# Where attention's ten weight conversions stand, and how many products of zeros open the kernel

## The chip, the cores and the metric

One of the eight cores of a Trainium2 chip runs the whole program. The metric is the time of one execution on the device in microseconds (us). The engines are TensorE (PE in the profile; its weight loads are PEld), VectorE (DVE), ScalarE (ACT), GpSimd (POOL) and SyncE (SP). Each engine works through its own instructions in a fixed order; an instruction whose input isn't there holds up all that stand behind it.

## The reference

Three layers follow each other. Attention has 4 batches, 8 heads, 576 positions and head width 64: the scores are `q k^T / 8`, a bias from the cumulated sums of `max(s, 0)` is added and clipped, the causal mask and a softmax follow, and the result is multiplied by `v`. The output, as 2304 rows of 512, goes through a layer of width 2048:

```python
h = x @ w_in
g = h * (1.0 / (1.0 + np.exp(-1.702 * h)))
x = g @ w_out
```

and then through a second one of the same sizes, with a rational function `P(h) / (Q(h) + 1e-6)` in place of the gate. The weights arrive as 64-bit floats.

## The kernel before

**Attention.** It is cut into 80 units: four batches, in each four pairs of heads, in each pair five tiles of rows, in the order 0, 1, 4, 2, 3. The loop in `attention` makes one step `j` per unit: it issues the scores of unit `j` (L289 on PE, the masked minimum L319 on DVE, the exponential L326 on ACT, the scaling by the inverse sum L339 on POOL), the transposes of unit `j - 3` (L360, L364, L381, copied out of PSUM at L361, L365, L385, L388) and the products with `v` of finished units (L406). In each pair the next pair's `k` and `q` are turned (L225) and split into a high and a low part (L213 on ACT, L216 on DVE, for the first two pairs moved by POOL at L251).

**Filler.** From batch 1 on PE has more to do than attention: `fill` deals out the first layer's work for the batch before (`mlp1_first`) in portions, three times per step. It begins at `j = 24`, with the products of the first five slices `f` of `w_in` (L638, with the gate at L649, L650, L652 and L655) for two halves of the rows, and then the products with the same five slices of `w_out` (`out1`, L662), from step 32 on: in each accumulation slice 0 comes first and slice 4 last, the first time at the end of step 33. Before `j = 24` `fill` only issues products of zeros (`warm`, L82) in the first five steps.

**Conversions.** The five slices need ten conversions of 128 x 512 weights from 64-bit floats to a high and a low 32-bit part (`convert`): the five halves of `w_in` first, then the five of `w_out` (`CONV`). One conversion is three instructions on ACT (L558, L560, and L566 that writes the high part), three on DVE (L561, L562, L563) and two on POOL (L565, and L567 that writes the low part). `emit` issues one after each step named in `CONV_J`. The raw weights come by a DMA on SP's queue (L547, L549) into one of three slots.

**Order.** In attention PE's order is the order of the code. On the other engines a scheduler places the instructions when the program is built. The eight PSUM banks serve all of it in turn.

**After attention.** The rest of the first layer and the second layer follow, with PE at work nearly all the time.

Of the kernel before, what the change touches and what calls it, by code (L numbers as in the profile page):

```python
# [47 lines left out]
PT_W = (256, 512, 768, 1024)  # L48
PARTS = ((0, 256), (256, 576))
ZEROS = 5  # L50
WARM = 6
RUN_ENDS = ((0, 1, 4, 2, 3), (4, 3), (4, 3), (3,))
W2_SLOTS = 7
LEAD = 2
CONV_J = (4, 6, 9, 12, 15, 18, 21, 24, 27, 30)
CONV = [(f, 0) for f in range(F1)] + [(f, 1) for f in range(F1)]
STG = 1536
BT_BUFS, G_BUFS = 9, 9
# [3 lines left out]
class Fused:  # L62
# [136 lines left out]
    def prep(self, att, b, p, ld, first=False):  # L199
# [48 lines left out]
        def move(o, i, hs=(0, 1)):  # L248
            if g < 2:
                for h in hs:  # L250
                    self.copied = nc.gpsimd.tensor_copy(o[:, h], i[:, h].bitcast(F32))  # L251
            else:
                nc.sync.dma_start(o.bitcast(F32), i.bitcast(F32))

        if first:
            turned = [[turn(nm, h) for nm in "kq"] for h in range(2)]
            for h in range(2):
# [7 lines left out]
                move(k2[h0, 1], qs[h0], (h,))  # L265
            self.warm(WARM)
            return
# [165 lines left out]
    def attention(self, att, mlp):  # L433
# [30 lines left out]
        for j in range(n + AHEAD + 1):  # L464
            i, k = j - AHEAD, j - AHEAD - 1
            self.zeros = j < ZEROS
            tr = iter(())
            if j < n:
                b, p, t = units[j]
                idx = j % 5  # L470
                if idx == 0 and units[j][1:] != (NP - 1, 0) or (idx == 0 and b + 1 < NB):
                    nprep = self.prep(att, *divmod(b * NP + p + 1, NP), loads.pop(b * NP + p + 1))
            if i >= 0 and i < n and units[i][0] and i % 20 == 1:
                self.filler = chain(self.filler, self.mlp1_first(mlp, units[i][0] - 1))
                self.cold = False
            q = FILL / 20
            if j < n:
                self.unit_scores(att, units[j], 0)
                if j:
                    next(nprep, None)  # L480
                if j == 2:
                    with self.behind((opened,)):
                        later.pop(0)()
                    with self.behind((self.moved,)):
                        self.raw_ahead()
            self.fill(q / 3, 1 if j else 4)
            if 0 <= i < n:
                tr = self.unit_transpose(att, units[i])
                next(tr, None)
            if j < n:  # L490
                self.unit_scores(att, units[j], 1)
            self.fill(q / 3, j < 4)
            for _ in tr:
                pass
            if j < n and idx == 4:
                for _ in nprep:
                    pass
                g = b * NP + p
                g = {0: 3, 1: 4, 2: NB * NP}.get(g, g + 2)
                if g < NB * NP:  # L500
                    with self.behind((opened,)):
                        loads[g] = self.pair_load(att, *divmod(g, NP))
                    later.append(loads[g]["values"])
            if k >= 0:
                run.append(units[k])
                if units[k][2] in RUN_ENDS[units[k][0]]:
                    for u in run:
                        self.unit_values(att, u)
                    run.clear()
                if units[k][2] == 3 and later:  # L510
                    later.pop(0)()
            self.fill(q / 3, j < 4)
            if j == AHEAD_J[0]:
                self.stg_n, self.stg_k = 0, 2
                buf = self.stg_slot[:, 2 * STG : 2 * STG + 1024].bitcast(F32R)
                buf = buf.rearrange("p (i f) -> p i f", i=2)
                for f in AHEAD_F:
                    for half in range(2):
                        self.task(
                            lambda st, f=f, half=half: self.park(st, buf, 1, f, half), 1, f, half  # L520
                        )
            if j in COEF_J:
                with self.behind((*self.tail, self.moved)):
                    if j == COEF_J[0]:
                        self.coefficients()
                    else:
                        self.nc.scalar.activation(self.cf[:, 6:8], self.cf[:, 4:6], AF.Abs)
            if j in CONV_J or j in AHEAD_J:
                with self.behind((*self.tail, opened)):
                    self.emit(1)  # L530
# [479 lines left out]
```

## Time and profile before

| | |
|---|---|
| three runs | 1022.36, 1023.72, 1023.92 us; median 1023.72 us |
| profiled execution | 1023.65 us, of which its span is 1021.7 us |
| PE busy | 1002.8 us, 98% of the span |
| DVE, ACT, POOL busy | 796.5, 718.8, 337.0 us |
| chain that ended last | PE 91%, DVE 4%, ACT 2%, DMA 1%, issue 1% |

The span runs from the first to the last instruction; the execution's own time is 1.95 us longer. The chain is followed back from the last instruction to what released each, so its shares say which engine the end waited for. A mean over the whole span hides that the first 80 us are another stage than the rest, so most rows below are of single stretches.

### The profile page before, as it was taken

Reading aid. Unit: us, or ns where it says so; the run is one execution under the profiler, and the core shown is the slowest. Engines: PE = TensorE matmul, PEld = TensorE weight load, DVE = VectorE, ACT = ScalarE, POOL = GpSimd, SP = SyncE. Lnnn points to the kernel's source line nnn. Section 1 sums busy time; section 2 is a strip of 40 time slices with the busy share of each in tenths; the row PEclk is TensorE's granted clock in tenths of the full one; section 3 lists DMA queues with packets and bytes.
Section 4 is the critical chain, followed back from the end, with each engine's and each line's share of the span. In section 5 each row is a group of like instructions: output and inputs, shape, how many; then the busy total and the mean of one; then the engine's idle time right before and its main releaser. Section 6 shows DMA issues by size and latency. Waiting matters only on the chain.

```text
span 1021.7 us, 19825 instructions
## 1 busy us (share of the span) xinstructions
PE 1002.8 (98%) x7053; PEld 936.4 (92%) x7054; DVE 796.5 (78%) x1804; ACT 718.8 (70%) x1661; POOL 337.0 (33%) x503
## 2 busy tenths in 40 slices
PE   8899999999999999999999999999999999999997
PEld 5678999999999999999999999999999999989896
DVE  7897667665537977777778747999998989889886
ACT  5999889878756655555555436777887777777775
POOL 5778656545410012222111112223222222222222
PEclk8999999999999999999999999999999999999999
DMA  7664465552228646766657635010010100100000
GB/s 182 150 166 104 131 179 148 153 140 72 53 97 274 183 126 197 234 222 231 222 176 239 207 124 208 1 31 32 1 62 1 32 31 1 63 1 1 32 1 31
DMA packets 79074, 115.97 MB, mean 114 GB/s; under 512 B 25552, under 2 KB 63072, under 8 KB 77440
## 3 DMA queue, kind: packets, MB, share of 16 engines
q1 hardware_dynamic: 72640, 94.94, 31.4%
q0 software_dynamic: 6112, 19.47, 5.1%
q8 instruction: 56, 0.92, 0.4%
q14 instruction: 42, 0.34, 0.1%
q10 hardware_dynamic: 224, 0.30, 0.1%
HBM read 74.78 MB, written 31.60 MB: 104 GB/s over the span
## 4 chain that ended last, share of the span: by engine, by line
PE 91%; DVE 4%; ACT 2%; DMA 1%; issue 1%; POOL 0%; ACTq 0%; SPq 0%; DVEq 0%
PE h L638 39%; PE a L815 19%; PE a L662 19%; PE s L289 5%; PE O L406 4%; PE tp L381 3%; DVE bt L319 1%; PE tk L225 1%; DMA x2p<-st 1%; PE tq L225 1%; PE tp L360 1%; DVE k L216 1%; PE idle L82 0%; ACT bt L326 0%; DMA raw<-in_moe_w_out_dram 0%
## 5 line engine op out<-in xcount | busy, mean ns | idle before, releaser
L638 PE MATMUL h<-x,u 128*128 128x288 f32 x1536 | 231.5, 296 | 1.0 <-ACT st L677 1.0
L662 PE MATMUL a<-gh,u 128*128 128x288 f32 x1024 | 231.8, 297 | 0.0
L638 PEld LDWEIGHTS h<-x,u 128*128 128x128 f32 x1536 | 212.8, 188 | 3.0 <-ACT st L677 1.3
L798 POOL TENSOR_TENSOR gl<-u,gh 128x384 fp32r<-128x384 f32 x96 | 105.6, 1100 | 289.8 <-ACT gh L796 265.5
L662 PEld LDWEIGHTS a<-gh,u 128*128 128x128 f32 x1024 | 173.0, 188 | 1.4 <-issue 0.5
L638 PE MATMUL h<-y,u 128*128 128x384 f32 x864 | 165.7, 336 | 0.0
L638 PEld LDWEIGHTS h<-y,u 128*128 128x128 f32 x864 | 152.9, 188 | 6.2
L662 PE MATMUL a<-gl,u 128*128 128x288 f32 x512 | 150.0, 295 | 0.1
L815 PE MATMUL a<-u,gh 128*128 128x512 f32 x432 | 114.6, 394 | 0.9 <-ACT gh L796 0.9
L649 ACT ACTIVATE g<-h 128x288 f32<-128x288 f32 x128 | 52.1, 408 | 78.5 <-PE h L638 77.8
L724 POOL DMA_DIRECT2D x<-xp x64 | 35.2, 551 | 207.4 <-DVE g L650 107.1
L662 PEld LDWEIGHTS a<-gl,u 128*128 128x128 f32 x512 | 96.5, 188 | 0.9 <-DVE gl L655 0.4
L326 ACT ACTIVATE bt<-bt,mn 128x128 f32<-128x128 f32 (+2 forms) x144 | 84.0, 584 | 18.6 <-DVE mn L319 17.3
L815 PEld LDWEIGHTS a<-u,gh 128*128 128x128 f32 x432 | 80.0, 188 | 14.9 <-ACT gh L796 1.8
L339 POOL TENSOR_SCALAR bt<-bt,sm 128x128 f32<-128x128 f32 (+2 forms) x144 | 81.7, 579 | 29.4 <-DVE sm L336 21.4
L796 ACT ACTIVATE gh<-u 128x384 fp32r<-128x384 f32 x96 | 50.6, 527 | 57.9 <-DVE u L794 57.9
L319 DVE CUSTOM_DVE_ANT_0 bt<-s,mask 128x128 f32<-128x128 f32 (+2 forms) x144 | 68.9, 481 | 28.3 <-PE s L289 26.4
L652 ACT ACTIVATE gh<-g 128x288 fp32r<-128x288 f32 x128 | 56.5, 443 | 45.4 <-DVE g L650 43.8
L650 DVE SCALAR_TENSOR_TENSOR g<-g,h 128x288 f32<-128x288 f32 x128 | 57.5, 450 | 30.1 <-ACT g L649 29.5
L781 ACT ACTIVATE y<-h,cf 128x384 f32<-128x384 f32 x96 | 55.4, 577 | 33.3 <-PE h L638 33.3
L786 DVE SCALAR_TENSOR_TENSOR y<-s,cf,y 128x384 f32<-128x384 f32 x96 | 59.2, 617 | 20.2 <-ACT s L783 18.8
L794 DVE SCALAR_TENSOR_TENSOR u<-y,u 128x384 f32<-128x384 f32 x96 | 73.4, 765 | 1.1
(116 smaller groups left out, 2054.2 us busy)
## 6 DMA issues: line engine op xcount, KB each, us to landing
raw<-in_moe_w_in_dram SPq DMA_DIRECT2D x24, 512.0 KB
raw<-in_moe_w_out_dram SPq DMA_DIRECT2D x24, 512.0 KB
x<-xp POOLq DMA_DIRECT2D x64, 144.0 KB, 3.0
wd<-park POOLq DMA_DIRECT2D x36, 256.0 KB, 4.4
u<-wd SPq DMA_DIRECT2D x8, 1024.0 KB
x2p<-st SPq DMA_DIRECT2D x32, 144.0 KB
xp<-x2p SPq DMA_DIRECT2D x32, 144.0 KB
xp<-x SPq DMA_DIRECT2D x32, 144.0 KB
```

The costliest lines, as they stand in the source:

```text
L319: nc.vector.tensor_tensor_reduce(bt[:, j0 : j0 + w], sc[:, :w], mask, 1.0, 3.0e38 if i == 0 else mn[:, 0:1], ALU.add, ALU.min, mn[:, i : i ...
L326: ex = nc.scalar.activation(bt[:, :n], bt[:, :n], AF.Exp, bias=mn[:, i : i + 1], scale=-1.0, accum_out=sm[:, col : col + 1],)
L339: nc.gpsimd.tensor_scalar(bt[:, :n], bt[:, :n], inv[:, i : i + 1], 1.0, ALU.mult, ALU.mult)
L638: nc.tensor.matmul(ps_tile, lhsT=u[:, wl, kk * P : (kk + 1) * P], rhs=x(xl, kk), start=(n == 0), stop=(n == 3 * KD - 1),)
L650: nc.vector.scalar_tensor_tensor(g[:, :w], g[:, :w], 1.0, h, ALU.add, ALU.mult)
L652: self.newest["act"] = nc.scalar.activation(gh[:, :w], g[:, :w], AF.Copy)
L662: nc.tensor.matmul(acc, lhsT=u[:, wl, d * P : (d + 1) * P], rhs=g[gl], start=(first and i == 0), stop=(last and i == 2),)
L781: nc.scalar.activation(y, h, AF.Abs, scale=cf[:, 4:5])
L786: nc.vector.scalar_tensor_tensor(y, s, cf[:, 7:8], y, ALU.mult, ALU.add)
L794: last = nc.vector.scalar_tensor_tensor(p, y, 2.0, p, ALU.subtract, ALU.mult)
L798: nc.gpsimd.tensor_tensor(gl, p, gh.bitcast(F32), ALU.subtract)
L815: nc.tensor.matmul(accs[m], lhsT=g[gl][:, m * P : (m + 1) * P], rhs=u[:, wl, :], start=(f == 0 and i == 0), stop=(f == NF - 1 and i == 2),)
```

## The change

`CONV_J` names later steps: four conversions instead of six stand in batch 0 (`j` below 20), and the last is issued in step 31 instead of 30. `WARM` puts eleven instead of six products of zeros behind the first pair's turns, and step 0 has seven instead of four between its two heads.

```diff
-WARM = 6
+WARM = 11
 ...
-CONV_J = (4, 6, 9, 12, 15, 18, 21, 24, 27, 30)
+CONV_J = (7, 11, 15, 19, 22, 25, 27, 28, 30, 31)
 ...
-            self.fill(q / 3, 1 if j else 4)
+            self.fill(q / 3, 1 if j else 7)
```

PE's order gains the eight products of zeros and is otherwise the same. ACT's, DVE's and POOL's are placed anew. In ACT's order before, around the first gate of the filler (`g<-h_0`, L649), the conversion that writes `u_1` is that of slice 1 of `w_out`, the seventh of ten; `bt` is a tile of attention's scores, named by pair, tile and head:

```order
L326 ACTIVATE bt_0_3_0_1307,sm_0_3_1306<-bt_0_3_0_1307,mn_0_3_0_1308 128x512
L388 COPY pt_0_1_1321<-tp_0_1_0_1322 128x512
L566 ACTIVATE u_1_508<-stgA 128x512
L649 ACTIVATE g<-h_0_1314 128x288
L326 ACTIVATE bt_0_3_1_1328,sm_0_3_1306<-bt_0_3_1_1328,mn_0_3_1_1329 128x512
```

The same place of the change, where `u_4` is slice 4 of `w_in`, the fifth conversion of ten:

```order
L388 COPY pt_0_1_1311<-tp_0_1_0_1312 128x512
L326 ACTIVATE bt_0_3_1_1318,sm_0_3_1306<-bt_0_3_1_1318,mn_0_3_1_1319 128x512
L566 ACTIVATE u_4_1250<-stgA 128x512
L649 ACTIVATE g<-h_0_1304 128x288
L213 ACTIVATE kh_2_1361<-tk_2_0_1365 64x288
```

Seven conversions have left ACT ahead of the filler's first gate before, and five now; behind it stand three before, and five now.

The second place is ACT's order where the last conversion, slice 4 of `w_out`, ends (`u_4`). Before:

```order
L652 ACTIVATE gh<-g 128x288
L566 ACTIVATE u_4_919<-stgA 128x512
L385 COPY pt_1_3_1899<-tp_1_3_0_1900 128x512
L416 ACTIVATE x_79<-O_1_0_1862 128x64
L326 ACTIVATE bt_2_4_0_1884,sm_2_4_1883<-bt_2_4_0_1884,mn_2_4_0_1885 128x576
L649 ACTIVATE g<-h_4_1892 128x288
```

And now:

```order
L326 ACTIVATE bt_2_4_0_1892,sm_2_4_1891<-bt_2_4_0_1892,mn_2_4_0_1893 128x576
L566 ACTIVATE u_3_1087<-stgA 128x512
L416 ACTIVATE x_79<-O_1_0_1861 128x64
L388 COPY pt_2_0_1958<-tp_2_0_0_1959 128x256
L649 ACTIVATE g<-h_4_1900 128x288
L326 ACTIVATE bt_2_2_0_1951,sm_2_2_1950<-bt_2_2_0_1951,mn_2_2_0_1952 128x384
L326 ACTIVATE bt_2_2_1_1963,sm_2_2_1950<-bt_2_2_1_1963,mn_2_2_1_1964 128x384
L566 ACTIVATE u_4_1250<-stgA 128x512
```

The last L566 moved from ahead of the exponential of tile 4 in the third pair to behind both exponentials of tile 2 of that pair, and the one before it (`u_3`) stands where the last one was left behind.

## Rows read from the trace of the kernel before

**Rows 1.** Busy us (instructions) of each engine by stretch; then clock, DMA share, GB/s.
```profile
core 0: us, PE busy (x) PEld busy (x) DVE busy (x) ACT busy (x) POOL busy (x), PEclk, DMA share, GB/s
11.97:18.70 6.73, 6.62 (x28) 5.33 (x28) 4.12 (x18) 3.75 (x13) 2.28 (x5) 0.50 0.78 203
18.70:24.00 5.30, 5.30 (x32) 3.56 (x32) 4.17 (x14) 3.25 (x9) 2.18 (x4) 0.99 0.89 258
24.00:82.80 58.80, 52.01 (x495) 41.05 (x494) 53.06 (x184) 57.69 (x164) 43.74 (x69) 1.00 0.61 156
82.80:118.70 35.90, 35.18 (x335) 33.57 (x335) 26.26 (x85) 34.13 (x99) 28.59 (x43) 1.00 0.46 121
118.70:1000.00 881.30, 880.12 (x6071) 836.77 (x6068) 686.00 (x1464) 604.66 (x1352) 247.01 (x358) 1.00 0.35 110
```

**Rows 2.** Timeline of PE in the opening: start, us, instructions, [idle before, releaser].
```profile
6.80 1.46 PE L82 MATMUL idle<-mask 128*128 128x512 bf16 x6
9.50 0.36 PE L289 MATMUL s<-k 68*128 68x256 f32 x1 [1.24 <-DMA k<-stgA]
...
9.83 1.04 PE L82 MATMUL idle<-mask 128*128 128x512 bf16 x4
11.79 0.42 PE L289 MATMUL s<-k 68*128 68x256 f32 x1 [0.93 <-POOL k L251]
...
12.68 1.08 PE L82 MATMUL idle<-mask 128*128 128x512 bf16 x2
```

**Rows 3.** Busy time and granted clock (PEclk) by the microsecond, columns as above.
```profile
11.00:12.00 1.00, 0.21 (x1) 0.19 (x1) 0.95 (x3) 0.00 (x0) 1.00 (x2) 0.97 0.01 3
12.00:13.00 1.00, 0.89 (x3) 0.46 (x3) 0.56 (x4) 0.45 (x2) 0.25 (x1) 0.50 0.67 140
...
18.00:19.00 1.00, 1.00 (x6) 0.97 (x7) 0.59 (x4) 0.59 (x2) 0.00 (x0) 0.62 0.70 154
19.00:20.00 1.00, 1.00 (x7) 0.73 (x7) 0.27 (x1) 0.99 (x3) 0.24 (x1) 1.00 0.66 150
```

**Rows 4.** Timeline of ACT from the filler's first gate on.
```profile
82.25 0.63 ACT L566 ACTIVATE u<-stgA 128x512 fp32r<-128x512 f32 x1
82.78 0.40 ACT L649 ACTIVATE g<-h 128x288 f32<-128x288 f32 x1
...
83.78 0.69 ACT L558 ACTIVATE stgA<-stgA 128x512 int32<-128x512 uint32 x1
84.35 0.66 ACT L560 ACTIVATE stgA<-stgA 128x512 f32<-128x512 f32 x1
84.92 0.41 ACT L213 ACTIVATE kh<-tk 64x288 fp32r<-64x288 f32 x1
...
107.91 0.67 ACT L558 ACTIVATE stgA<-stgA 128x512 int32<-128x512 uint32 x1
...
111.67 0.51 ACT L326 ACTIVATE bt<-bt,mn 128x256 f32<-128x256 f32 x1
...
118.17 0.60 ACT L326 ACTIVATE bt<-bt,mn 128x384 f32<-128x384 f32 x1
```

**Rows 5.** The ten conversions on POOL, by line, 24 to 120 us: busy, mean ns | idle before.
```profile
L567 POOL TENSOR_TENSOR u<-stgA,u 128x512 fp32r<-128x512 f32 x10 | 13.4, 1343 | 2.4 <-ACT u L566 2.3
L565 POOL TENSOR_TENSOR stgA<-stgA 128x512 int32<-128x512 int32 x10 | 13.0, 1304 | 6.3 <-DVE sm L336 3.5 <-DVE stgA L563 1.5 <-ACT pt L388 1.1
```

**Rows 6.** The chain that ended last, 24 to 80 us, shares by line.
```profile
by line: issue 14.0%; DVE bt L319 9.4%; PE O L406 8.6%; PE s L289 8.1%; ACT bt L326 7.3%; DVE k L216 7.2%; PE tp L381 5.3%; DVE stgA L563 4.5%; POOL u L567 4.1%; DMA vn<-in_v_dram 3.9%; DVE qs L216 3.8%; DVE stgA L561 3.1%; POOL bt L339 3.0
```

**Rows 7.** Timeline of POOL, the end of the tenth conversion.
```profile
116.58 1.31 POOL L567 TENSOR_TENSOR u<-stgA,u 128x512 fp32r<-128x512 f32 x1
```

**Rows 8.** Timeline of PE where slice 4 of `w_out` is first used.
```profile
117.89 0.29 PE L662 MATMUL a<-gh,u 128*128 128x288 f32 x1
...
120.16 0.30 PE L662 MATMUL a<-gh,u 128*128 128x288 f32 x1
```

## The prediction

> **What bounds the kernel now.** I read the page first: PE is busy for 98% of the span and has 91% of the chain, so time is won only where PE stands still, works at a low clock, or gets more work. The table of stretches shows where that is [rows 1]. From 118.7 to 1000 us PE is busy for 880.12 of 881.30 us: what comes before that is handed through to the end one for one, and nothing there can take it up. From 24.0 to 82.8 us, attention's batch 0 up to the filler's first gate, PE is busy for 52.01 of 58.80 us, and ACT for 57.69, 98%: ACT sets the pace, DVE with 53.06 close behind. From 82.8 to 118.7 us PE is busy for 35.18 of 35.90 us, so PE sets the pace, but ACT has only 1.77 us free (35.90 - 34.13). From 11.97 to 18.70 us PE is busy for 6.62 of 6.73 us at a granted clock of 0.50, the lower of its two levels (1.2 GHz against 2.4).
>
> **The opening.** Ahead of that stretch PE stands for 1.24 us until the first scores' sums have landed and for 0.93 us until POOL has moved a part of the second head [rows 2]. The clock then falls near 12 us and is back in the 19th microsecond [rows 3]. The change fills these gaps. A product of zeros takes 0.243 us there (1.46 / 6), so five more take 1.22 of the 1.24 us; three more at 0.26 us (1.04 / 4) take 0.78 of the 0.93 us [rows 2]. I cost them at nothing: the wait for the DMA and for POOL hides them. Should the clock be low when they run, each takes 0.54 us (1.08 / 2), eight take 4.3 us, and 4.3 - 2.2 = 2.1 us of that stand in front of the scores.
>
> What can be won is the low clock from 11.97 to 18.70 us. If all of PE's 6.62 us there ran twice as fast, 3.3 us would go. DVE, which takes each score out of PSUM, has 4.12 us of work in the same 6.73 us, and would be late next: no more than 6.73 - 4.12 = 2.6 us can go [rows 1]. The lower end is nothing, if the clock falls in spite of the zeros. The three runs of before lie 1.56 us apart, with one 1.36 us under the median; I read that, without proof, as an execution that was spared the low clock, and take 2.0 us, between 1.36 and 2.6. From 18.7 to 24 us DVE is busy for 4.17 of 5.30 us, so the lead isn't lost there at once.
>
> Here a page speaks against the change. The row shows one execution whose clock fell after two gaps of about a microsecond. The Trainium skill (TensorE: Matmul & The Clock Gate, Part 1) says that how many matmuls a kernel runs slowly at its start differs from run to run. By that rule the 2.0 us would be won in some executions and not in others, and a median could stand anywhere between 1021.0 and 1023.0 us; by the row it is won in each. The spread of 1.56 us doesn't contradict it; one profiled execution can't show it.
>
> **Two conversions out of batch 0.** Seven conversions have left ACT before the filler's first gate in the old order, five in the new. On ACT one takes 0.57 + 0.57 + 0.53 = 1.67 us of its time, start to start [rows 4], so ACT has 3.34 us less to do from 24 to 82.8 us. ACT is the bound there, so 3.3 us is the most. The chain gives the other end: in 56 us the three lines L563, L567 and L561 alone have 4.5 + 4.1 + 3.1 = 11.7%, 6.6 us, for the seven conversions, 0.94 us each [rows 6]; two of them make 1.9 us. ACT's 98% lies nearer to the upper end; I take 2.9 us. PE's room for it is there: it stands still for 6.79 us of that stretch. POOL loses 2 x 2.65 us (1.343 + 1.304) [rows 5] and isn't missed, as it is idle for 15 of 58.8 us. SP's order is moved with it: the loads of raw weights come later and nearer to use. Each is a transfer of 512 KB at a stage where the DMA share is 0.46 to 0.61, so I cost that at nothing, and at about a microsecond of ACT's time where one is late.
>
> **The same two in batch 1.** They come back between the filler's first gate and the first use of slice 4 of `w_out`. There ACT is given 3.34 us more and has 1.77 us free, so it falls behind by at least 1.57 us; POOL is given 5.3 us and has 7.31 us free (35.90 - 28.59). The new order of ACT places the last L566 behind the exponential that starts at 118.17 us [rows 4]. Without any idle time ACT's work from 82.8 us up to the end of that L566 is 34.13 + 3.34 = 37.5 us, so it ends at 120.3 us of the old time, and L567 1.34 us later, at 121.6 us. PE needs the low part at 120.16 us [rows 8]; in the old order it was there at 116.58 + 1.31 = 117.89 us [rows 7]. So 1.5 us of standing, and as PE stands for 0.72 us in this stretch already, 0.8 us where it takes that wait's place. The other end is the time that the tenth conversion takes from its first instruction to its last, 107.91 to 117.89 us, 10.0 us [rows 4, 7]. The new order begins it behind the exponential that ends at 111.67 + 0.51 = 112.18 us [rows 4], 4.3 us later; with these and ACT's 1.57 us it ends at 123.8 us, and PE stands for 3.6 us. I take the middle, 2.2 us. What stands behind a late L566 on ACT are exponentials and gates, for which PE waits too; the 2.2 us hold that.
>
> **Sum.** For the profiled execution's own time of 1023.65 us: -2.0 (opening) - 2.9 (batch 0) + 2.2 (batch 1) = -2.7 us, so 1021.0 us. The median of the three runs, 1023.72 us, is 0.07 us above that execution, which changes nothing. The two conversion terms together run from -3.3 + 0.8 = -2.5 to -1.9 + 3.6 = +1.7 us.
>
> **Rivals.**
>
> *The clock falls all the same.* Only the conversions' -0.7 us are left: 1023.0 us. For it: the first fall came after a stretch that was mostly transposes and waits, and those stay. Against it: the two waits shown are filled nearly whole. The page's rule above belongs to this case, as it makes it true for a part of the executions.
>
> *ACT's lead is kept.* The opening gives its bound of 2.6 us and the conversions theirs of 2.5 us: 1018.5 us. For it: PE has idle time enough in batch 0, and attention works three units ahead of its transposes. Against it: ACT has nearly no free time left up to 118 us.
>
> *The conversions starve the filler stage (slower).* Five conversions now stand between the first gate and slice 4's use, and in POOL's queue each puts an L565 of 1.30 us and an L567 between the scaling steps (L339) that PE's transposes wait for. If PE can't fill the time of one such instruction per conversion, 5 x 1.30 = 6.5 us go, and with the 1.5 us at slice 4's use 8.0 us; less 2.0 and 2.9 us this is 1023.65 + 3.1 = 1026.8 us. It decides from a loss of 4.9 us in that stage on. For it: POOL's free time there shrinks from 7.3 to 2.0 us. Against it: before, with three conversions in the stage, PE stood for 0.72 us in all.
>
> **How the numbers follow.** The forecast has 0.52, with a range of its own from 1019.5 to 1022.5 us; the clock's fall 0.18; the kept lead 0.17; the starved stage 0.13. A measurement of this kernel can tell about 0.2%, 2.05 us, from no change: faster is below 1021.67 us, slower above 1025.77 us. Faster holds three quarters of the forecast (0.39) and the kept lead (0.17): 0.56. Slower is the worse part of the starved stage, 0.08. The rest, 0.36, is within 0.2%. The range of 8 in 10 is 1018.6 to 1024.0 us: it takes in the first rival, nearly all of the forecast and half of the second, and leaves out most of the third (0.09 + 0.11 = 0.2).
>
> **What would show it.** In the profile after, the granted clock should stay at 1.00 from 12 to 19 us and the scores should start at 9.5 us as before; if they start later, the zeros are in the way. The filler's first gate should stand about 4.9 us earlier, near 77.9 us. PE should then stand for about 2 us more between the gate and the first products with `w_out`, with POOL's L567 or ACT's L566 as the releaser; from there to the end nothing should change. I am wrong if the gate isn't earlier by at least 3 us, or if PE stands for over 5 us in batch 1.

## The result, and the profile after

The changed kernel takes 1028.73 us, median of five runs (1027.91 to 1030.38), where the kernel before took 1023.72 us (1022.36 to 1025.12, five runs). The ratio is 1.0053 with a 95% interval of 1.0040 to 1.0066: slower by about 5 us. I had forecast 1021.0 us. The profiled execution took 1030.38 us with a span of 1028.4 us, 6.7 us more than before's.

Where these 6.7 us arise is seen best from three instructions that each kernel has: the first product of the filler (L638), the first product with `w_out` (L662), and attention's last turn of a weight block (L225, `tq`). The view of one line's instructions gives their first and last start. Before:

```profile
L638 PE MATMUL h<-x,u x1536: 288/294/403, 79.9 to 609.4; 128*128 128x288 f32 x192
...
L662 PE MATMUL a<-gh,u x1024: 288/295/402, 115.4 to 615.5; 128*128 128x288 f32 x171
...
L225 PE MATMUL tq<-ident,qn x84: 243/246/303, 6.0 to 258.5; 96*128 96x96 f32 x84
```

After:

```profile
L638 PE MATMUL h<-x,u x1536: 288/294/405, 76.6 to 616.1; 128*128 128x288 f32 x192
...
L662 PE MATMUL a<-gh,u x1024: 288/295/609, 115.0 to 622.2; 128*128 128x288 f32 x171
...
L225 PE MATMUL tq<-ident,qn x84: 243/246/302, 5.5 to 265.0; 96*128 96x96 f32 x84
```

| us | before | after | difference |
|---|---|---|---|
| up to the filler's first product | 79.9 | 76.6 | -3.3 |
| from there to the first product with `w_out` | 35.5 | 38.4 | +2.9 |
| from there to the last turn | 143.1 | 150.0 | +6.9 |
| from there to the end of the span | 763.2 | 763.4 | +0.2 |

So 3.3 us were won up to the filler's first product, and lost twice behind it: 2.9 us in the filler's first stage, and 6.9 us behind the first product with `w_out`. The stretches of [rows 1], of after, same columns:

```profile
11.97:18.70 6.73, 5.73 (x39) 4.47 (x40) 4.76 (x21) 4.98 (x16) 3.01 (x6) 1.00 0.81 213
...
24.00:82.80 58.80, 53.91 (x500) 43.14 (x499) 49.89 (x173) 54.94 (x158) 37.62 (x67) 0.97 0.59 145
82.80:118.70 35.90, 32.92 (x306) 30.98 (x305) 29.78 (x81) 33.45 (x94) 27.88 (x39) 1.00 0.44 116
118.70:1000.00 881.30, 876.57 (x6044) 833.34 (x6045) 682.52 (x1463) 602.06 (x1346) 249.77 (x361) 1.00 0.35 112
```

The clock of the opening is 1.00 instead of 0.50, as forecast. But from 24.0 to 82.8 us it is 0.97, where it had been 1.00; PE stands for 2.98 us from 82.8 to 118.7 us instead of 0.72 us, and for 4.73 us behind that instead of 1.18 us. The timeline of PE names the places:

```profile
80.14 1.34 PE L638 MATMUL h<-x,u 128*128 128x288 f32 x8 [1.11 <-DVE x L417]
...
104.16 0.30 PE L364 MATMUL tp<-ident,bt 128*64 128x128 f32 x1 [0.80 <-DVE mn L319]
...
107.37 1.06 PE L638 MATMUL h<-x,u 128*128 128x288 f32 x6 [1.38 <-ACT pt L361]
...
117.73 0.40 PE L662 MATMUL a<-gh,u 128*128 128x288 f32 x1 [0.35 <-ACT u L566]
...
121.92 0.61 PE L662 MATMUL a<-gh,u 128*128 128x288 f32 x1 [3.66 <-POOL u L567]
122.46 3.26 PE L406 MATMUL O<-pt,vn 128*64 128x128 f32 x28
```

Three waits of 3.29 us together stand in the filler's first stage; before, two of 0.72 us together did. At 117.7 and 121.9 us PE waits for both halves of one slice of `w_out`, 4.01 us together, and then works at half the clock: the 28 products of L406 take 3.26 us (1.75 us in before). Busy time and granted clock (the third number from the end) by the microsecond show this, and the low clock in batch 0:

```profile
28.00:29.00 1.00, 1.00 (x10) 0.67 (x11) 0.94 (x5) 1.00 (x5) 0.23 (x1) 0.55 0.94 161
...
31.00:32.00 1.00, 1.00 (x9) 0.98 (x8) 0.72 (x4) 0.08 (x1) 0.73 (x3) 0.74 0.58 109
...
119.00:120.00 1.00, 0.00 (x0) 0.00 (x0) 0.76 (x4) 1.00 (x4) 1.00 (x1) 1.00 0.90 317
120.00:121.00 1.00, 0.00 (x0) 0.00 (x0) 0.16 (x1) 0.76 (x3) 0.83 (x3) 0.63 0.04 14
...
127.00:128.00 1.00, 1.00 (x8) 0.96 (x7) 0.77 (x2) 0.00 (x0) 0.00 (x0) 0.95 0.53 118
```

The clock falls in the 29th microsecond and is back in the 32nd; it falls again during the standing, in the 121st, and is back in the 128th.

What PE waited for is the conversion of slice 3 of `w_out`, the ninth of ten. ACT's timeline: the gate, the beginnings of the ninth and tenth conversion, and their L566.

```profile
81.03 0.39 ACT L649 ACTIVATE g<-h 128x288 f32<-128x288 f32 x1
...
108.29 0.67 ACT L558 ACTIVATE stgA<-stgA 128x512 int32<-128x512 uint32 x1
...
112.58 0.69 ACT L558 ACTIVATE stgA<-stgA 128x512 int32<-128x512 uint32 x1
...
117.02 0.65 ACT L566 ACTIVATE u<-stgA 128x512 fp32r<-128x512 f32 x1
...
120.24 0.63 ACT L566 ACTIVATE u<-stgA 128x512 fp32r<-128x512 f32 x1
```

POOL's timeline of their second half:

```profile
115.51 1.31 POOL L565 TENSOR_TENSOR stgA<-stgA 128x512 int32<-128x512 int32 x1
116.77 2.19 POOL L655 TENSOR_TENSOR gl<-g,gh 128x288 fp32r<-128x288 f32 x2
118.92 1.28 POOL L565 TENSOR_TENSOR stgA<-stgA 128x512 int32<-128x512 int32 x1
...
120.60 1.26 POOL L567 TENSOR_TENSOR u<-stgA,u 128x512 fp32r<-128x512 f32 x1
```

Slice 3's high half is ready at 117.67 us, so its L567 could have begun then. In POOL's order it stands behind two subtractions of the filler (`gl`, L655), which end at 118.96 us, and behind L565 of slice 4, and it ends at 121.86 us. From its first instruction to its last the conversion takes 13.6 us; the tenth of before took 10.0 us [rows 4, 7].

### The profile page after: what moved, and what is told of

The parts are those of the page before. It is cut to its first block, busy times and chain, and to the rows that moved or that the text cites. A ratio compares the mean times of both kernels' runs of the same rounds, so it can differ in the third digit from the quotient of the medians.

```text
span 1028.4 us, 19842 instructions
## 1 busy us (share of the span) xinstructions
PE 1005.6 (98%) x7061; PEld 938.1 (91%) x7062; DVE 800.2 (78%) x1804; ACT 719.2 (70%) x1661; POOL 336.8 (33%) x503
## 4 chain that ended last, share of the span: by engine, by line
PE 89%; DVE 3%; ACT 3%; DMA 2%; issue 1%; POOL 1%; SPq 0%; ACTq 0%; DVEq 0%; POOLq 0%
PE h L638 38%; PE a L815 19%; PE a L662 18%; PE s L289 5%; PE O L406 4%; PE tp L381 3%; ACT bt L326 1%; DMA k<-qs 1%; PE tp L360 1%; DMA x2p<-st 1%; PE tk L225 1%; PE tq L225 1%; DMA raw<-in_moe_w_out_dram 0%; DVE bt L319 0%; DMA k<-stgA 0%
## 5 line engine op out<-in xcount | busy, mean ns | idle before, releaser
L662 PE MATMUL a<-gh,u 128*128 128x288 f32 x1024 | 232.7, 298 | 4.0 <-POOL u L567 3.7
L638 PE MATMUL h<-x,u 128*128 128x288 f32 x1536 | 231.8, 296 | 3.6 <-ACT pt L361 1.4
L638 PEld LDWEIGHTS h<-x,u 128*128 128x128 f32 x1536 | 212.9, 188 | 6.0 <-ACT pt L361 1.6
L662 PEld LDWEIGHTS a<-gh,u 128*128 128x128 f32 x1024 | 173.4, 188 | 6.1 <-POOL u L567 3.9
L638 PE MATMUL h<-y,u 128*128 128x384 f32 x864 | 165.7, 336 | 0.0
L638 PEld LDWEIGHTS h<-y,u 128*128 128x128 f32 x864 | 152.9, 188 | 6.2
L662 PE MATMUL a<-gl,u 128*128 128x288 f32 x512 | 150.1, 295 | 0.4 <-DVE gl L655 0.4
L815 PE MATMUL a<-u,gh 128*128 128x512 f32 x432 | 114.6, 394 | 0.9 <-ACT gh L796 0.9
L649 ACT ACTIVATE g<-h 128x288 f32<-128x288 f32 x128 | 52.2, 409 | 79.8 <-PE h L638 79.1
L662 PEld LDWEIGHTS a<-gl,u 128*128 128x128 f32 x512 | 96.6, 189 | 1.2 <-DVE gl L655 0.7
L650 DVE SCALAR_TENSOR_TENSOR g<-g,h 128x288 f32<-128x288 f32 x128 | 57.5, 450 | 31.7 <-ACT g L649 31.2
```

The lines of the kernel that those rows point to most:

```text
L638: nc.tensor.matmul(ps_tile, lhsT=u[:, wl, kk * P : (kk + 1) * P], rhs=x(xl, kk), start=(n == 0), stop=(n == 3 * KD - 1),)
L650: nc.vector.scalar_tensor_tensor(g[:, :w], g[:, :w], 1.0, h, ALU.add, ALU.mult)
L662: nc.tensor.matmul(acc, lhsT=u[:, wl, d * P : (d + 1) * P], rhs=g[gl], start=(first and i == 0), stop=(last and i == 2),)
L815: nc.tensor.matmul(accs[m], lhsT=g[gl][:, m * P : (m + 1) * P], rhs=u[:, wl, :], start=(f == 0 and i == 0), stop=(f == NF - 1 and i == 2),)
```

## The experiments

Late is the stretch from the first product with `w_out` to the last turn, 143.1 us before; stage is the one ahead of it, 35.5 us before. Each line's ratio is against the kernel before on the same chip; late, stage and gate (the first L649) are of the profiled execution.

| kernel | median us (lowest to highest) | ratio, 95% interval | gate | stage | late |
|---|---|---|---|---|---|
| before | 1023.72 (1022.36 to 1025.12) | | 82.8 | 35.5 | 143.1 |
| after | 1028.73 (1027.91 to 1030.38) | 1.0053, 1.0040 to 1.0066 | 81.0 | 38.4 | 150.0 |
| e1_zeros | 1024.39 (1021.46 to 1025.83) | 1.0005, 0.9996 to 1.0015 | 80.9 | 35.5 | 143.1 |
| e2_conv | 1030.71 (1029.36 to 1032.14) | 1.0070, 1.0058 to 1.0082 | 81.0 | 38.4 | 150.0 |
| e3_earlier_end | 1023.71 (1023.19 to 1024.64) | 1.0000, 0.9992 to 1.0009 | 81.7 | 38.3 | 143.1 |
| e4_two_late | 1027.60 (1026.87 to 1029.57) | 1.0043, 1.0030 to 1.0055 | 83.0 | 35.5 | 147.7 |
| e5_zeros_in_wait | 1027.61 (1027.02 to 1028.11) | 1.0043, 1.0028 to 1.0058 | 81.1 | 38.3 | 147.8 |
| e6_pool_to_dve | 1023.05 (1022.07 to 1023.77) | 0.9998, 0.9989 to 1.0007 | 82.0 | 38.2 | 143.1 |
| e7_act_to_dve | 1024.47 (1022.65 to 1025.32) | 1.0010, 1.0001 to 1.0020 | 81.0 | 38.9 | 143.1 |
| e8_slice4_last | 1023.22 (1022.00 to 1024.45) | 0.9996, 0.9987 to 1.0005 | 82.4 | 37.0 | 144.8 |
| e9_fifth_earlier | 1022.55 (1021.10 to 1023.79) | 0.9990, 0.9981 to 0.9999 | 80.6 | 37.3 | 143.1 |
| e10_zeros_longer | 1026.10 (1024.85 to 1027.69) | 1.0019, 1.0008 to 1.0031 | 84.3 | 36.2 | 143.1 |
| e11_even | 1029.24 (1028.36 to 1030.74) | 1.0052, 1.0038 to 1.0066 | 89.4 | 38.5 | 143.1 |
| e12_e9_old_zeros | 1022.14 (1021.22 to 1024.15) | 0.9983, 0.9973 to 0.9993 | 78.9 | 37.2 | 143.1 |

### The two parts apart, and the late end

**e1_zeros** keeps the new zeros and puts the old steps back.

```diff
-CONV_J = (7, 11, 15, 19, 22, 25, 27, 28, 30, 31)
+CONV_J = (4, 6, 9, 12, 15, 18, 21, 24, 27, 30)
```

> The products of zeros alone; the conversions stand as before. Theory L (the halves of w_out converted last come too late, PE stands for slice 3 and its clock falls behind it): the opening won 2.2 us in the changed kernel's trace (the transposes of unit 0 start at 18.30 instead of 20.48 us) and keeps that here, 1021.5 us. Rival Z (the zeros only shift PE's idle time, and the clock that fell near 28 us in the changed kernel is their doing): 1023 to 1025 us, with a low clock somewhere before 40 us.

The median lies in the rival's range; its 0.5 us can't be told from nothing. Its profiled execution, the shortest of its twelve at 1021.46 us, has a clock of 1.00 in all stretches and is 2.2 us below before's. PE's waits there stand 1.9 us earlier than before's, and do so to the end of batch 0. The first and the last of ten in PE's timeline of before:

```profile
25.26 0.66 PE L360 MATMUL tp<-ident,bt 128*128 128x128 f32 x4 [0.68 <-POOL bt L339]
...
77.22 0.68 PE L381 MATMUL tp<-ident,bt 128*128 128x128 f32 x2 [0.41 <-POOL bt L339]
```

And of e1_zeros:

```profile
23.37 0.66 PE L360 MATMUL tp<-ident,bt 128*128 128x128 f32 x4 [0.76 <-POOL bt L339]
...
75.31 0.68 PE L381 MATMUL tp<-ident,bt 128*128 128x128 f32 x2 [0.38 <-POOL bt L339]
```

The mean clock of each execution says why the median doesn't follow: two of the twelve were at 0.999 or more (1021.46 and 1022.24 us), the other ten at 0.996 or 0.997 (1023.50 to 1025.83 us). Of 23 runs of before on that chip six were. In these runs the zeros didn't make full speed more frequent.

**e2_conv** is the other part alone.

```diff
-WARM = 11
+WARM = 6
 ...
-            self.fill(q / 3, 1 if j else 7)
+            self.fill(q / 3, 1 if j else 4)
```

> The conversions alone; the zeros stand as before. Theory L: all of the loss is here, the changed kernel's +5.0 us and the 2.2 us of the opening besides, 1030 to 1031 us, with PE standing for 3 to 4 us at slice 3 of w_out. Rival Z: half the loss belongs to the zeros, 1026 us.

It costs 7 us, so the new steps hold the whole loss. Its ratio is 0.0017 above after's, 1.7 us that the zeros may be worth there; but the two intervals overlap. PE's waits in batch 0 are the same as in after. First of after, whose opening was at full clock:

```profile
27.26 0.52 PE L381 MATMUL tp<-ident,bt 128*128 128x128 f32 x3 [1.41 <-DVE k L216]
44.09 0.66 PE L381 MATMUL tp<-ident,bt 128*128 128x128 f32 x4 [0.46 <-POOL bt L339]
```

Then of e2_conv, whose opening was at the low clock up to 18 us:

```profile
28.76 0.52 PE L381 MATMUL tp<-ident,bt 128*128 128x128 f32 x3 [1.41 <-DVE k L216]
44.10 0.66 PE L381 MATMUL tp<-ident,bt 128*128 128x128 f32 x4 [0.46 <-POOL bt L339]
```

At 27 us after is 1.5 us ahead, at 44 us 0.01 us. Between them lies after's low clock from 28 to 31.7 us: a fall near 28 us took all that the zeros had won in the opening.

These are single executions. In none of the ten profiled ones with the new zeros did the clock fall near 12 us, and with the old zeros it did in three of four (before, e2_conv, e12_e9_old_zeros). But between 27 and 35 us it fell in six of the ten (after, e6, e8, e9, e10, e11), and in e4_two_late too, which has the old zeros and ran its opening at full clock. So a fall near 28 us doesn't need the new zeros.

**e3_earlier_end** is after with the last five conversions moved a step or two forward, so that none is issued right behind the ninth.

```diff
-CONV_J = (7, 11, 15, 19, 22, 25, 27, 28, 30, 31)
+CONV_J = (7, 11, 15, 19, 22, 24, 26, 27, 28, 30)
```

> The changed kernel with its second half of conversions a little earlier: steps 24, 26, 27, 28, 30 instead of 25, 27, 28, 30, 31; batch 0 and the zeros as changed. Theory L: slice 3 is ready two steps sooner, PE no longer stands for it and the clock stays, so the 4.0 us of waiting and the 2.4 us of low clock go: 1022 to 1024 us. Rival C (five conversions crowd ACT, DVE and POOL between steps 22 and 31 and the wait at slice 3 is only where that shows): as many conversions stand in the stage, PE stands for as long but earlier, 1027 to 1029 us.

Late is 143.1 us again, with no wait of PE from 114 to 124 us, and the median that of before. At like clock it may be a little slower: its six runs at 0.999 or more took 1023.19 to 1023.85 us, before's six 1022.41 to 1023.64 us. The 5 us hang on the last five steps. The stage stays long, and the gate is only 1.1 us earlier than before's.

**e4_two_late** is the kernel before with its last two conversions in steps 30 and 31 alone.

```diff
-CONV_J = (4, 6, 9, 12, 15, 18, 21, 24, 27, 30)
+CONV_J = (4, 6, 9, 12, 15, 18, 21, 24, 30, 31)
```

> The kernel before with only its last two conversions (w_out slices 3 and 4) issued in steps 30 and 31 instead of 27 and 30. Theory L: PE stands about 4 us at slice 3 and the clock falls, 1028 to 1030 us. Rival C: one more conversion in a stage that has been relieved in step 27, no more than 1 us: 1023.7 to 1024.7 us.

Two numbers make before 4.4 us slower (1.0043), with a stage of 35.5 us as before: the loss behind the first product with `w_out` needs neither five conversions in the stage nor the zeros. PE's timeline has the same wait, shorter, with 0.33 us for L566 ahead of it:

```profile
123.49 0.61 PE L662 MATMUL a<-gh,u 128*128 128x288 f32 x1 [2.33 <-POOL u L567]
```

### What the 6.9 us are, and who starves the stage

**e5_zeros_in_wait** is after with products of zeros in PE's wait for slice 3, to see what the time is if the clock doesn't fall there.

```diff
+                if blk == 0 and d == 0 and f == 3:
+                    self.idle_bank = self.bank("M", "idle2")
+                    self.warm(16)
```

> The changed kernel with sixteen more products of zeros (16 x 0.216 = 3.5 us at the high clock) in PE's order just ahead of slice 3 of w_out, where PE stood for 4.0 us. Theory L with the clock as a second cost: the wait stays, but the clock doesn't fall behind it, and the stretch from the first product with w_out to the last turn (146.9 us in the changed kernel, 140.0 before) comes to 144.3 us; the time falls by 2 to 3 us, to 1025.5 to 1026.5 us. If the wait alone cost the 6.9 us, the stretch stays at 146.9 us or grows, 1028 to 1029 us.

The expectation counts the stretch from a later start than the table, 3.1 us shorter: its 146.9, 140.0 and 144.3 us are 150.0, 143.1 and 147.4 us here. PE's timeline shows the same end of the wait, and L406 at full speed:

```profile
117.25 3.63 PE L82 MATMUL idle<-mask 128*128 128x512 bf16 x15
...
121.99 0.40 PE L662 MATMUL a<-gh,u 128*128 128x288 f32 x1 [0.84 <-POOL u L567]
122.31 1.75 PE L406 MATMUL O<-pt,vn 128*64 128x128 f32 x28
```

The clock doesn't fall, and late is 147.8 us: of the 6.9 us the standing is 4.7, the low clock behind it 2.2. That is read from two traces. The median falls by 1.1 us only, where I expected 2 to 3, and the intervals of the two ratios overlap.

**e6_pool_to_dve** and **e7_act_to_dve** ask who makes the stage long. Both are e3_earlier_end, and take work of the last five conversions to DVE: e6 POOL's two instructions each, e7 ACT's L566.

```diff
-        eng = nc.vector if self.stg_slot is None else nc.gpsimd
+        eng = nc.vector if self.stg_slot is None or self.late else nc.gpsimd
```

```diff
-        nc.scalar.activation(hi, x, AF.Copy)
+        if self.late:
+            nc.vector.tensor_copy(hi, x)
+        else:
+            nc.scalar.activation(hi, x, AF.Copy)
```

> The conversions at steps 7, 11, 15, 19, 22, 24, 26, 27, 28, 30 (as in e3_earlier_end), but the two instructions of POOL in each of the last five are put on DVE. The open 2.8 us are those by which the stretch from the filler's first product to the first with w_out grew (35.5 to 38.3 us). If POOL's queue, or DVE and POOL hindering each other, is the cause: 36 to 37 us, and 1022 us. If ACT is the cause: 38.3 us, 1023.7 us; if DVE is made the bound by it: 39 us or more, 1025 us.

> The same conversions, but the last of ACT's three instructions (L566, 0.53 us of ACT's time) in each of the last five is put on DVE: 2.7 us less for ACT between the filler's first product and the first with w_out. If ACT is what holds that stretch up (34.13 of 35.90 us busy before, with 3.34 us more to do now): 36 us instead of 38.3 us and 1021.5 us. If POOL or DVE is the cause: 38 us or more, 1023.7 to 1024.5 us.

From 82.8 to 118.7 us POOL's busy time falls to 22.21 us in e6 (32.80 us in e3), and the stage is 38.2 us instead of 38.3. In e7 ACT's falls to 31.37 us (33.90 us in e3), and the stage grows to 38.9 us. By the expectations e6 points at ACT, and e7 at POOL or DVE. Taking POOL's share of the conversions or L566 away doesn't shorten the stage. But both load DVE more (34.20 and 31.62 us, 29.23 in e3), so a gain on POOL or ACT may have been lost again on DVE, and none of the three engines is ruled out.

**e8_slice4_last** leaves only the tenth conversion late.

```diff
-CONV_J = (7, 11, 15, 19, 22, 25, 27, 28, 30, 31)
+CONV_J = (7, 11, 15, 19, 22, 24, 26, 27, 28, 31)
```

> The changed kernel with slice 3 of w_out early (step 28) and slice 4 alone as late as in the change (step 31): steps 24, 26, 27, 28, 31. Theory L with slice 3 as the culprit: slice 3 costs nothing, slice 4 is used half a step later, and its low part, with no other conversion beside it, is ready about 1 us after its use: 1024 to 1025 us. If step 31 is too late by itself: PE stands 3 to 4 us at slice 4 with the low clock behind it, 1028 to 1029 us.

From 114 to 124 us PE then stands once, at slice 4, and the clock holds behind it:

```profile
120.28 0.40 PE L662 MATMUL a<-gh,u 128*128 128x288 f32 x1 [1.34 <-POOL u L567]
```

Late is 144.8 us, 1.7 us more than before, and the median doesn't show it. What I had priced in batch 1, slice 4 at step 31, was there and of about the forecast's size. In after it can't be seen, since PE is held up at slice 3 first.

### The gate, and a better version

DVE's timeline of after explains the wait of 1.11 us at 80.14 us. The fifth conversion, from step 22, has its three instructions just there, ahead of the `x` (L417) that the filler's products wait for:

```profile
77.46 0.42 DVE L561 TENSOR_SCALAR stgA<-stgA 128x512 f32<-128x512 f32 x1
...
78.39 0.69 DVE L563 SCALAR_TENSOR_TENSOR stgA<-stgA 128x512 int32<-128x512 int32 x1
79.00 0.68 DVE L319 CUSTOM_DVE_ANT_0 bt<-s,mask 128x512 f32<-128x512 f32 x1
79.68 0.40 DVE L417 TENSOR_TENSOR x<-O,x 128x256 fp32r<-128x256 f32 x1
```

**e9_fifth_earlier** moves it to step 20, with the two before it spread out.

```diff
-CONV_J = (7, 11, 15, 19, 22, 25, 27, 28, 30, 31)
+CONV_J = (7, 11, 14, 17, 20, 24, 26, 27, 28, 30)
```

> As e3_earlier_end, but the third to fifth conversion at steps 14, 17, 20 instead of 15, 19, 22, so that none of DVE's three instructions of the fifth stands ahead of the last pair's x (L417), for which PE stood 1.10 us in the filler's first product. If that queue took back the relief of batch 0: the wait goes, the filler's first gate comes at 80.0 to 80.7 us instead of 81.7 us, and the time is 1022.5 us. If ACT's whole load up to the gate sets it: the gate stays at 81.7 us or comes later, since no work is taken away, 1023.7 us.

The wait is gone, the stage is 1.0 us shorter than e3_earlier_end's, and the ratio falls by 0.001, which is within the two intervals. The first product with `w_out` isn't earlier in its trace (115.2 us, 114.6 in e3): there the clock fell from 29 to 33 us, and in e3's it didn't. **e12_e9_old_zeros** gives that kernel the old opening (the same diff as in e2_conv).

> The conversions of e9_fifth_earlier (1022.55 us) with the kernel before's zeros (six and four). If the zeros bring nothing in the median, as e1_zeros said: 1022 to 1023 us, and the gain of e9_fifth_earlier belongs to its conversions. If they are worth the 1.7 us by which the changed kernel and e2_conv differ: 1024.2 us, no better than before.

Its median is 1.7 us below before's (0.9983), and further below after's. The gate stands at 78.9 us, 3.9 us earlier than before. Of PE's waits from 75 to 125 us these are all:

```profile
83.90 0.47 PE L225 MATMUL tq<-ident,qn 96*128 96x96 f32 x3 [0.65 <-ACT pt L361]
103.77 0.71 PE L225 MATMUL tq<-ident,qn 96*128 96x96 f32 x6 [0.23 <-DVE g L650]
111.24 0.63 PE L381 MATMUL tp<-ident,bt 128*128 128x128 f32 x4 [1.15 <-DVE qs L216]
```

They are 2.03 us, 1.3 us more than before's 0.72 us.

But the gate's 3.9 us aren't all the steps' doing. In this execution the low clock of the opening lasted from the 13th to the 16th microsecond only, in before's to the 19th, and PE's first transposes (L381) came 1.8 us earlier. Before, then e12_e9_old_zeros:

```profile
20.48 0.38 PE L381 MATMUL tp<-ident,bt 128*128 128x128 f32 x2
```

```profile
18.69 0.38 PE L381 MATMUL tp<-ident,bt 128*128 128x128 f32 x2
```

Counted from the first transposes, the opening drops out. In these five executions, and in those of e5 and e7, the clock didn't fall between there and the first product with `w_out`:

| us from the first transposes to | before | e1_zeros | e2_conv | e3_earlier_end | e12_e9_old_zeros |
|---|---|---|---|---|---|
| the filler's first product | 59.44 | 59.52 | 56.77 | 56.82 | 57.51 |
| the first gate | 62.30 | 62.39 | 61.14 | 62.26 | 60.20 |
| the first product with `w_out` | 94.95 | 95.05 | 95.08 | 95.18 | 94.71 |

The new steps bring the filler's first product 1.9 to 2.7 us nearer, and at the first product with `w_out` no more than 0.2 us of that is left (e5 and e7: 95.28 and 95.93 us). So by these traces what batch 0 gains, the stage takes, and nearly all of e12's gain lies ahead of the first transposes or in the clock. Five of its ten runs had a mean clock of 0.999 or more (1021.22 to 1022.18 us), and one of fifteen of before beside it (1022.25 us). It was so with either opening: six of e9's eleven and six of e3's eleven with the new zeros, against five of nineteen and six of 23 of before. Why full speed is more frequent with the new steps isn't shown.

Two tries missed. **e10_zeros_longer** is e1_zeros with up to eight zeros and at all three places of a step.

```diff
-ZEROS = 5
+ZEROS = 8
 ...
-            self.fill(q / 3, j < 4)
+            self.fill(q / 3, 1)
```

> The conversions as before, the changed kernel's zeros, and one product of zeros at each of the three places of every step up to step 7 instead of up to step 3 or 4. If the zeros of the change brought nothing in the median since in most executions the clock falls a little later instead (near 28 us, as the changed kernel's trace showed, when PE stood idle for 1.4 us behind step 6): the clock stays in nearly all of them, 1021.5 to 1022.5 us and a narrower spread than e1_zeros (1021.46 to 1025.83). If the spread has another cause: 1024.4 us as e1_zeros, or 0.5 to 1 us more for the added products.

It is slower (1.0019), and the clock still falls, at 29.9 us. PE waits for 1.79 us at 27.42 us, with DVE's L361 as the releaser. Whether the zeros hold a PSUM bank too long there I didn't test.

**e11_even** has e10's zeros and evenly spaced conversions.

```diff
-CONV_J = (7, 11, 15, 19, 22, 25, 27, 28, 30, 31)
+CONV_J = (6, 8, 11, 13, 16, 18, 20, 23, 26, 29)
```

> The zeros of e10_zeros_longer, and conversions at steps 6, 8, 11, 13, 16, 18, 20, 23, 26, 29: the first later than before, so that the opening is free of them, the last ones earlier, so that none is late for the products with w_out, and seven ahead of the filler. By what the runs showed so far, conversions in batch 0 and in batch 1 cost about the same, and only late ones cost more: 1021 to 1022.5 us, within 0.5 us of e10_zeros_longer. If relief of the opening steps is worth something: 1 us or more below it.

Eight conversions come ahead of its gate instead of seven; the gate is at 89.4 us (84.3 in e10), PE waits for 1.36 us for `x` ahead of it, and the clock falls twice, at 31 and at 89 us. The ratio is 1.0052; what the loss is made of I didn't separate.

## Why the prediction was wrong

**The step that failed is "the same two in batch 1", with "I take the middle, 2.2 us".** I followed slice 4 alone, the last conversion, and priced its L566 and L567. The standing came at slice 3, which the change moves to step 30 with slice 4 on its heels: POOL's order puts slice 4's L565 ahead of slice 3's L567. Each slice is used by three products, and the first row of [rows 8], at 117.89 us, is the one that needs slice 3's low half: it is due 2.27 us ahead of slice 4's, and 2.46 us behind the first product with `w_out`. In after that is 117.5 us, and the half was ready at 121.86 us; the clock fell in the standing. That is 4.7 + 2.2 us instead of 2.2 us (e5), and e4 shows that two late conversions alone do it. Had slice 3's conversion, begun at 108.29 us, taken the 10.0 us of [rows 4, 7], it would have ended at 118.3 us, 0.8 us late; the other 3.6 us are its lengthening to 13.6 us. This is an estimate: no run has slice 3 at step 30 without slice 4 behind it. My own term, slice 4's, measured 1.7 us in e8, inside its bounds of 0.8 to 3.6 us.

**Two conversions out of batch 0, -2.9 us.** The size holds at the filler's first product: counted from the first transposes it is 2.7 us nearer in e2_conv than in before, and in e3_earlier_end than in e1_zeros. But the gate is only 1.2 us nearer in e2 and 0.1 us in e3 (in after it stood 1.8 us earlier, 81.0 us against 82.8): I had counted ACT's relief and left out what DVE has ahead of the products, and the fifth conversion stood in front of `x` there. With e9's steps and the old zeros (e12) the gate is 2.1 us nearer. By the first product with `w_out` nothing of it is left in e2 and e3, and 0.2 us in e12; the sum's batch 1 term priced only the end of that stage.

**The opening, -2.0 us.** Its trace came out as said: clock 1.00 from 12 to 19 us, and the first transposes (L381) at 18.30 us instead of 20.48 us, by this row of after:

```profile
18.30 0.38 PE L381 MATMUL tp<-ident,bt 128*128 128x128 f32 x2
```

In e1's profiled execution, at full clock throughout, the time is 2.2 us below before's. But before has such executions too (six of 23 were at 0.999 or more), and e4's opening ran at full clock with the old zeros:

```profile
18.12 0.38 PE L381 MATMUL tp<-ident,bt 128*128 128x128 f32 x2
```

In the median I find no gain from the zeros (e1: 1.0005), and in after's trace it doesn't add to the conversions' gain; the 1.7 us between after and e2_conv stay open, and e9 and e12 don't show them. So this term failed too, though not on the way to the 5 us. I had given 0.18 to the clock falling all the same; it did, at 28 instead of 12 us. The page weighed in the prediction comes near this: the Trainium skill (TensorE: Matmul & The Clock Gate, Part 1) has the number of slow matmuls at a kernel's start differ from run to run. The mean clocks of e1's twelve runs, 0.996 to 1.000, fit it, but don't say where in each run the clock was low; the traces show falls at 12 us, near 28 us, or none.

**The rivals.** The starved stage, to which I gave 0.13, was nearest: 1026.8 us, and its condition, a loss of 4.9 us or more in the stage up to slice 4's use, was met: from the first gate to there it was 37.4 us before (82.78 to 120.16 us) and 45.3 us after (81.03 to 126.29 us), 7.9 us more against its 8.0 us. That the sizes agree is in part luck: it had POOL's instructions between the scaling steps in mind, and most of the loss was the standing at slice 3 and the clock. Its own mechanism isn't borne out by e6, where these instructions are off POOL and the stage stays, nor ruled out, as they load DVE there. Of the stage's 2.9 us, 1.11 us are the wait for `x`: e3 has it, e9 hasn't, and e9's stage is 1.0 us shorter. Who causes the other two waits, 0.80 and 1.38 us, isn't settled. "Five conversions in the stage" fits all of e3, e6, e7, e8 and after (37.0 to 38.9 us) against three (35.5 us in before, e1 and e4, 36.2 in e10), but e11 has 38.5 us with two, with a low clock from 89 to 93 us in it, and no run has separated their number from their places.

**What would show it.** "I am wrong if the gate isn't earlier by at least 3 us", 1.8 us, "or if PE stands for over 5 us in batch 1": 3.29 us in the stage and 4.01 us at slice 3. Both came.

## What to carry to other kernels

When a row of jobs is pushed later, price each job against its own first use, not only the last one; two jobs issued back to back interleave on an engine that works in order, and the earlier one then ends late. A wait on TensorE can cost more behind it: in after the standing took 4.7 us and the low clock after it 2.2 us, while in e8 a wait of 1.34 us was followed by full clock. A fall of the clock that is taken out of one place must be looked for at the next, and judged by many executions, not by one trace. Where the start of a kernel varies, count from a point behind it: from the first transposes the best kernel here is 0.2 us ahead of before at the first product with `w_out`, though counted from the span's start it is 2.0 us ahead (113.4 against 115.4 us).

## What the runs showed of the hardware

DVE's steps of a conversion can get longer when one of POOL's runs beside them. In after, L561 takes 0.42 us with POOL idle (at 77.46 us), and here, with POOL at work:

```profile
98.42 1.32 DVE L561 TENSOR_SCALAR stgA<-stgA 128x512 f32<-128x512 f32 x1
...
101.70 1.79 DVE L563 SCALAR_TENSOR_TENSOR stgA<-stgA 128x512 int32<-128x512 int32 x1
```

POOL's rows beside these:

```profile
98.15 1.30 POOL L565 TENSOR_TENSOR stgA<-stgA 128x512 int32<-128x512 int32 x1
...
101.67 1.28 POOL L567 TENSOR_TENSOR u<-stgA,u 128x512 fp32r<-128x512 f32 x1
```

L561 goes from 0.42 to 1.32 us, and L563 from 0.69 us (at 78.39 us) to 1.79 us; POOL's own 1.30 and 1.28 us stay as they were [rows 5]. In both pairs POOL started first. In e3 there are two in which DVE did, and there it is POOL that takes longer: L567 takes 1.72 us at 103.09 us, behind an L563 of 0.70 us at 102.95 us, and in these rows 1.79 us, while L563 keeps its 0.68 us:

```profile
83.40 0.68 DVE L563 SCALAR_TENSOR_TENSOR stgA<-stgA 128x512 int32<-128x512 int32 x1
```

```profile
83.44 1.79 POOL L567 TENSOR_TENSOR u<-stgA,u 128x512 fp32r<-128x512 f32 x1
```

The Trainium skill (GPSIMD Engine Reference, 1. Specifications) says that GpSimd shares its SBUF interfaces with VectorE, with contention for certain DVE instructions, among them those with two SBUF inputs. L563 has two, and its rows above agree. In e6, with POOL's instructions gone from the late conversions, L561's mean from 80 to 122 us is 508 ns (766 ns in e3), L563's 735 ns (772 ns in e3). Conversions beside POOL's work can thus cost DVE more than their own lengths; how much of the stage's growth that is I can't say.
